# Four transformer layers on one core: the same operations in another written-out order, with fewer and longer bursts of small matrix products

## The chip, the core and the metric

The kernel runs on one NeuronCore of a Trainium2 chip. A core has a matrix engine (TensorE, in the profile PE, its weight loads PEld), a vector engine (VectorE, DVE), a scalar engine (ScalarE, ACT), a general engine (GpSimd, POOL) and a queue that starts DMAs (SyncE, SP). Each engine works through its own queue in order; semaphores tie the queues together. SBUF is the on-chip memory of 128 partitions, PSUM the eight banks into which PE writes. The metric is the device time of the whole program in microseconds.

## The reference

The input x has 2048 tokens of width 448. Two kinds of layer alternate, A B A B, each with a layer norm ahead and a residual sum behind:

```python
# A: 16 heads of width 28, each token looks at 8 tokens: itself and 7 at steps of 2 back
qkv = (x @ wqkv).reshape(B, S, 3, H, Dh)
idx = pos[:, None] - (arange(8) * 2)[None, :]
logits = einsum("bhsd,bhswd->bhsw", q, kg) * Dh**-0.5   # masked where idx < 0
o = einsum("bhsw,bhswd->bhsd", softmax(logits), vg)
return o @ wo
# B: gated, F = 1792
h = (x @ w_gate) * (x @ w_up)
return h @ w_down
```

All inputs and the output are bf16. Both A layers share their weights, and both B layers theirs.

## The kernel before, in words

Tokens lie in SBUF so that those of even and of odd place form the two halves of the token axis; a step of 2 back is then a step of 1 inside a half. A layer is worked in chunks of 256 or 512 tokens (`CH`, `SEQ`), and the chunks of neighbouring layers overlap: layer 1 begins while layer 0 still has chunks to do.

**Layer norm** (`ln_chunk`): DVE takes the statistics (L578, L580), ACT makes 1/sqrt (L581, L583), DVE normalises (L599). The transposition goes by PE (L609, L613) with an evacuation on ACT or DVE (L620, L623) in layer 0, and by DMA later.

**Projections** (`qk_chunk`, `v_group`): whole products of 64 rows by 128 columns, in pairs that fill the two halves of the array. All whole products are issued at L347. Evacuations of q and k are L708, of v L773 to L800; the `ORDER` list decides whether ACT or DVE does each.

**Attention** (`attn_front`, `attn_back`): the query blocks (17 of 120 or 128 queries) go in 9 groups, one of one block and eight of two. For a group of two, PE makes 32 + 32 small score products (L831; half as many where the tiles are 64 by 64), ACT takes the exponential (L841), DVE puts the band mask on (L848). Then PE makes 32 + 32 small value products (L866; 16 + 16 for the single block), whose results are copied (L880, ACT or DVE), added (L884), and normalised: a shuffle of the sums on DVE (L894), logarithm and exponential on ACT (L895, L896), the product on DVE (L907). The output projection and residual sum follow (`y_blocks`, L924). The small products use tiles of 64 rows by 32 columns; the scores of the first six groups of layer 0 use 64 by 64.

**The gated layer** (`b_chunk`): 14 hidden units of 128 features for each chunk. A unit is seven pairs of whole products (gate and up), an ACT copy of the gate (L960) and a DVE product with the up half (L963). The down projection is again in pairs at L347, its residual sum is L924; the last two token blocks use L975 and L979.

**What sets the order.** Nothing is planned when the program is built. `ORDER` (L101) is a written list of operation numbers for each engine, and `BANKS` (L163) names the PSUM banks of each PE operation. `schedule` (L222) reads both; it adds a wait on the operation that empties a bank to the next one that takes it. `emit` (L271) issues the queues and sets a semaphore wait where an operation reads what another engine wrote. An entry of the PE list such as

```python
"805+806*845/3/2"
```

is a **burst with strips**: the small products of operations 805 and 806 are issued together, and three of the seven steps of the whole operation 845, from its third step on, are spread between them. Those steps are then not one pair of products of 128 columns but eight products of 32 columns at four places in each half of the array, issued at L350 (`pair`, L342), so that the tiling does not change inside the burst. `cut_of` (L359) cuts the small products into parts of eights around the strips. An entry that is one number, such as `866`, is issued as it stands; `a+b*c/k/f` gives the bursts a and b, the host c, its strip steps k, and the step f from which they are taken.

Of the kernel before, what the change touches and what calls it, by code (L numbers as in the profile page):

```python
# [93 lines left out]
def grp_nc(g):  # L94
# [22 lines left out]
    ),  # L117
    "act": (
# [12 lines left out]
    ),  # L131
    "dve": (
# [18 lines left out]
    ),  # L151
    "pool": (
        "21 24 39 28 23 18 29 35 40 25 36 26 20 32 44 33 37 19 27 22 41 34 38 42 30 65 43 31 63"
# [952 lines left out]
```

## Time and profile before

| | us |
|---|---|
| median of 3 runs | 384.64 |
| lowest, highest | 384.35, 386.83 |
| the profiled execution | 384.78 |
| its span in the trace | 382.8 |
| PE busy | 377.2 |
| DVE busy | 288.7 |
| ACT busy | 197.2 |

The span runs from the first to the last instruction of the trace; the profiled execution took 2.0 us more than that. "Busy" is the time in which at least one instruction of an engine ran. For PE the ends of matmuls are modelled, so that starts are the better guide to what a product costs; the timeline view gives them. In the grouped views a row has the line, engine, operation, tiles and shapes, the count, then the busy time and the mean duration in ns, and behind the second bar the idle time of the engine ahead of it with what ended it.

### The profile page before, as it was taken

The numbers are of one execution on the slowest core, as the hardware profiler recorded it, in microseconds if no ns is written. First come the engines' busy times: TensorE is split into PE (matmuls) and PEld (weight loads), VectorE is DVE, ScalarE is ACT, GpSimd is POOL, SyncE is SP. The second block draws the span as 40 slices with busy tenths as digits, with TensorE's granted clock in tenths as the row PEclk, the third lists the DMA queues.
The fourth block names the chain that finished last, engine by engine and source line by source line (L and its number), as shares of the span: only waits on it lengthen the run. The fifth ranks groups of instructions, "written<-read, shape, count | busy, mean of one in ns | idle before, by whom it ended". The sixth has DMA issues, their size and how long they took to land.

```text
span 382.8 us, 14279 instructions
## 1 busy us (share of the span) xinstructions
PE 377.2 (99%) x6338; PEld 210.8 (55%) x6338; DVE 288.7 (75%) x652; ACT 197.2 (52%) x383; POOL 7.1 (2%) x33
## 2 busy tenths in 40 slices
PE   8999999999999999999999999999999999999997
PEld 3655577544454545446766666555555444445665
DVE  7998999998756876897567888668899687174443
ACT  4897887566426356156456236448653534125220
POOL 6000000000000000000000000000000000000000
PEclk9999999999999999999999999999999999999999
DMA  7665542700421030232001214320124002313004
GB/s 251 171 161 135 122 116 65 105 3 2 81 39 39 11 56 19 50 62 47 6 15 38 50 29 76 73 36 8 35 46 75 2 3 60 64 23 38 2 2 134
DMA packets 54880, 22.49 MB, mean 59 GB/s; under 512 B 45012, under 2 KB 54820, under 8 KB 54820
## 3 DMA queue, kind: packets, MB, share of 16 engines
q1 hardware_dynamic: 54676, 21.53, 26.5%
q8 instruction: 50, 0.82, 0.9%
q14 instruction: 10, 0.08, 0.1%
q10 hardware_dynamic: 144, 0.06, 0.1%
HBM read 8.54 MB, written 2.71 MB: 29 GB/s over the span
## 4 chain that ended last, share of the span: by engine, by line
PE 89%; DVE 6%; DMA 1%; ACT 1%; issue 1%; SPq 0%; DVEq 0%
PE ps L347 81%; PE ps L350 3%; PE ps L831 2%; PE ps L866 2%; PE ps L975 1%; DVE st L578 1%; DMA xnTb<-xn_sb 1%; DVE xn_sb L599 1%; DVE E_sb L848 1%; DVE x_sb L924 1%; DMA x_sb<-in_A_x_dram 1%; DVE oT L907 0%; PE ps L613 0%; DVE hT L963 0%; DVE R_sb L894 0%
## 5 line engine op out<-in xcount | busy, mean ns | idle before, releaser
L347 PE MATMUL ps<-xnTb,WGU 64*128 64x512 bf16 (+1 forms) x1900 | 173.7, 332 | 0.3
L347 PEld LDWEIGHTS ps<-xnTb,WGU 64*128 64x128 bf16 x1900 | 92.4, 94 | 71.5 <-ACT g_sb L960 1.5
L960 ACT ACTIVATE g_sb<-ps 128x512 bf16<-128x512 f32 (+1 forms) x140 | 69.0, 509 | 112.4 <-PE ps L347 93.8
L963 DVE TENSOR_TENSOR hT<-g_sb,ps 128x512 bf16<-128x512 bf16 (+1 forms) x140 | 77.7, 573 | 43.2 <-ACT g_sb L960 41.8
L347 PE MATMUL ps<-WD,hT 64*128 64x448 bf16 x802 | 83.5, 349 | 0.1
L347 PEld LDWEIGHTS ps<-WD,hT 64*128 64x128 bf16 x802 | 38.5, 94 | 33.4 <-DVE hT L963 0.5
L347 PE MATMUL ps<-xnTa,WQK 64*128 64x512 bf16 (+1 forms) x486 | 52.7, 352 | 0.6 <-issue 0.3
L924 DVE TENSOR_TENSOR x_sb<-x_sb,ps 128x448 bf16<-128x448 bf16 x62 | 36.8, 611 | 18.2 <-PE ps L347 18.1
L841 ACT ACTIVATE E_sb<-ps,shift_sb 128x1024 bf16<-128x1024 f32 (+1 forms) x36 | 37.5, 1068 | 11.6 <-PE ps L831 11.4
L578 DVE BATCH_NORM_STATS2 st<-x_sb 128x6 f32<-128x448 bf16 x64 | 38.5, 615 | 1.5 <-DMA x_sb<-in_A_x_dram 1.3
L599 DVE TENSOR_SCALAR xn_sb<-x_sb,mv,rstd 128x512 bf16<-128x512 bf16 (+1 forms) x64 | 35.1, 567 | 4.7 <-ACT rstd L583 4.5
L347 PEld LDWEIGHTS ps<-xnTa,WQK 64*128 64x128 bf16 x486 | 23.4, 94 | 18.4 <-issue 0.4
L708 ACT ACTIVATE qk<-ps 128x1024 bf16<-128x1024 f32 (+1 forms) x28 | 25.7, 929 | 8.7 <-PE ps L347 6.1
L347 PE MATMUL ps<-wo_g,oT 64*128 64x448 bf16 x256 | 29.5, 350 | 0.1
L895 ACT ACTIVATE R_sb<-R_sb 128x480 f32<-128x480 f32 (+1 forms) x34 | 19.9, 601 | 15.7 <-DVE R_sb L894 15.6
L848 DVE TENSOR_TENSOR E_sb<-E_sb,MK 128x1024 bf16<-128x1024 bf16 (+1 forms) x36 | 23.1, 656 | 5.2 <-ACT E_sb L841 5.2
L907 DVE TENSOR_TENSOR oT<-O_sb,R_sb 128x480 bf16<-128x480 f32 (+3 forms) x36 | 21.8, 624 | 6.5 <-ACT R_sb L896 6.5
L347 PE MATMUL ps<-WV,xnTa 64*128 64x336 bf16 (+3 forms) x252 | 23.3, 304 | 0.0
L894 DVE STREAM_SHUFFLE R_sb<-O_sb 128x480 f32<-128x480 f32 (+1 forms) x34 | 22.8, 691 | 0.0
L896 ACT ACTIVATE R_sb<-R_sb 128x480 f32<-128x480 f32 (+1 forms) x34 | 19.9, 599 | 0.2
L347 PEld LDWEIGHTS ps<-wo_g,oT 64*128 64x128 bf16 x256 | 12.1, 94 | 11.1 <-DVE oT L907 0.7
L866 PEld LDWEIGHTS ps<-E_sb,v_sb 64*32 64x32 bf16 x1088 | 12.6, 90 | 8.2 <-issue 3.6
(61 smaller groups left out, 215.4 us busy)
## 6 DMA issues: line engine op xcount, KB each, us to landing
out_dram<-x_sb SPq DMA_DIRECT2D x15, 112.0 KB, 1.8
x_sb<-in_A_x_dram SPq DMA_DIRECT2D x3, 448.0 KB, 5.7
hT<-in_A_wqkv_dram SPq DMA_DIRECT2D x4, 224.0 KB, 4.8
WGU<-in_B_w_gate_dram SPq DMA_DIRECT2D x4, 224.0 KB, 4.0
WGU<-in_B_w_up_dram SPq DMA_DIRECT2D x4, 224.0 KB, 4.4
WD<-in_B_w_down_dram SPq DMA_DIRECT2D x2, 448.0 KB, 4.9
WGU<-in_B_w_gate_dram SPq DMA_DIRECT2D x2, 336.0 KB, 4.6
WGU<-in_B_w_up_dram SPq DMA_DIRECT2D x2, 336.0 KB, 4.4
```

The source lines that it names most:

```text
L347: return lambda E: E.matmul(out(), lhs(), rhs(), start=start, stop=stop)
L578: sc.add("dve", one(lambda E, B=B: E.bn_stats(st6[:, B, :], x_sb[:, B, :]), ("bn", li, B)), 525.0, deps=[("x", li - 1, B)] + ([("xn", li - ...
L599: sc.add("dve", one(lambda E, B=B, dst=dst, src=src: E.tensor_scalar(dst, src, mv[:, B, 0:1], rstd[:, B:B + 1], ALU.subtract, ALU.mult), ( ...
L708: return E.activation(dst, src, ACT.Copy) if hasattr(E, "activation") else E.tensor_copy(dst, src)
L841: return E.activation(E_sb[:, slot, 2 * hp:2 * hp + 2, 0:w], ps[:, b0:b0 + 2, 0:w], ACT.Exp, bias=shift_sb[:, 0:1], scale=SCALE)
L848: return E.tensor_tensor(e, e, MK[:, kind, 0:nc].unsqueeze(1).unsqueeze(1).to_broadcast([128, 2, w // nc, nc]), ALU.min)
L866: parts[eb // 2].append((lambda E, b=b, c=c, o=o, vw=vw, eb=eb, eo=eo: E.matmul(ps[32 * b:32 * b + 32, bk[c], o:o + nc], vw, E_sb[64 * c:6 ...
L894: sc.add("dve", one(lambda E: E.stream_shuffle(R_sb[:, rs, 0:w], O_sb[:, os_, 0:w], [DH] * 32), ("Rs", li, qb)), dve_est(w) + 20.0, deps=[ ...
L907: return E.tensor_tensor(oT[:, :, a % HALF:a % HALF + z - a], O[:, :, a - tok:z - tok], R_sb[:, rs, 0:w].rearrange("p (h n) -> p h n", h=4 ...
L924: sc.add("dve", one(lambda E: E.tensor_tensor(x_sb[:, B, :], x_sb[:, B, :], ps[:, bk[w], 0:D], ALU.add), ("x", li, B)), dve_est(D), deps=[ ...
L960: sc.add("act", one(lambda E, gs=gs, bk=bk: E.activation(g_sb[:, gs, 0:nt], ps[:, bk[0], 0:nt], ACT.Copy), ("G", li, j, fc)), act_est(nt), ...
L963: sc.add("dve", one(lambda E, gs=gs, bk=bk, fc=fc: E.tensor_tensor(hT[:, fc, hs, 0:nt], g_sb[:, gs, 0:nt], ps[:, bk[1], 0:nt], ALU.mult), ...
```

## The change

The lists `ORDER` and `BANKS` are replaced; no other line differs. The program issues the same operations. What is different:

- PE's queue. Small products stand in 38 bursts instead of 45. The value products of three and of four blocks now stand in one burst (one of 96 and two of 128 products, at most 64 before), with five or seven strip steps between. In all there are 54 strip steps instead of 58. Some bursts mix score and value products in both kernels. The places of projections, hidden units, and output products between the bursts move too.
- DVE's and ACT's queues follow another order, and 43 evacuations change between the two engines. DVE has 11 of the 36 q and k copies (8 before), 5 of the v copies of L800 (8 before) and 17 of the 36 first copies of value sums (14 before).
- SP's queue of DMAs is in another order; so are the PSUM banks. GpSimd's queue is the same.

From the diff of `ORDER`'s PE list (the other lists are replaced in the same way):

```diff
-        "805+806*845/3/2 863 857 869 848 875 860 872 922 881 923 935 940 936 941 916 1003 917 920 1015 1006 921 1012 918 818 919 1027 819 1024 1039 1018 1036 "
-        "854 1030 946+947*866/2/1 878 884 952 1009 953 970+971*885/2/5 890 886 1042 887 1021 891 965 892 976 1033 977 893 966 1045 1061 1064 1070 1046 1067 1073 "
...
-        "1234 1240 1104 1237 1185+1186*1105/3/4 1167 1168*1106/2 1306 1310 1307 1311 1252 1308 1191+1192*1312/2 1309 1313 1330 1180 1331 1181 1341+1342*1246/2/5 "
+        "805+789+806+790*860/5 845 857 869 881 863 872 920 922 921 923 935 918 875 916 936 919 917 1012 1003 940 1006 941 1024 946*854/1/6 947 866 1018 1015 818 "
+        "1030 819 952+953*878/2/5 1027 1009 1036 1039 884 1021 970+971*885/2 890 886 887 976+977*891/2/4 1033 892 1042 893 1064 1070 1067 965 1061 1073 966 1045 "
...
+        "1234 1228 1185+1186*1105/2/1 1106 1231 1243 1240 1306 1312 1191+1167+1192+1168*1307/3/1+1313/4 1246 1252 1255 1308 1258 1309 1310 1237 1311 1330 1180 "
```

Here 789, 790 and 805, 806 are the value products of the first group (one block) and the second group (two blocks) of layer 2, whose 96 products now stand in one burst; 1167, 1168 and 1191, 1192 are those of its groups 4 and 5, now 128 products in one burst.

122 rows, old and new, of tables (BANKS, ORDER) are left out of this document.

## The prediction

> **What bounds the kernel now.** I read the page first: the span, the busy shares, the slices and the chain that ended last.
>
> ```profile
> span 382.8 us, 14279 instructions
> PE 377.2 (99%) x6338; PEld 210.8 (55%) x6338; DVE 288.7 (75%) x652; ACT 197.2 (52%) x383; POOL 7.1 (2%) x33
> ...
> DVE  7998999998756876897567888668899687174443
> ...
> PE 89%; DVE 6%; DMA 1%; ACT 1%; issue 1%; SPq 0%; DVEq 0%
> PE ps L347 81%; PE ps L350 3%; PE ps L831 2%; PE ps L866 2%; PE ps L975 1%; DVE st L578 1%; DMA xnTb<-xn_sb 1%; DVE xn_sb L599 1%; DVE E_sb L848 1%; DVE x_sb L924 1%; DMA x_sb<-in_A_x_dram 1%; DVE oT L907 0%; PE ps L613 0%; DVE hT L963 0%; DVE R_sb L894 0%
> ```
>
> PE is busy for 99% of the span and makes 89% of the chain, so the time is the sum of PE's work. But DVE's slices are nearly full for the first quarter, so I then asked for busy time by stretches (columns: stretch, its length, then busy us and instruction count of each engine):
>
> ```profile
> 12.00:95.00 83.00, 81.96 (x1692) 47.78 (x1690) 79.15 (x197) 63.10 (x115) 0.00 (x0) 1.00 0.42 90
> 95.00:300.00 205.00, 204.90 (x3614) 114.14 (x3612) 155.43 (x334) 103.25 (x200) 0.00 (x0) 1.00 0.23 42
> ```
>
> From 12 to 95 us PE and DVE are both full: DVE has 83.00 - 79.15 = 3.85 us to spare, and PE's idle of 83.00 - 81.96 = 1.04 us is where it already waits. From 95 to 300 us PE is idle for 0.1 us and DVE has 49.6 us to spare: there only PE's own order counts, and the waits of an order that leaves too little between a product and its reader. The granted clock is 1.00 in both.
>
> "Busy" hides what a burst of small products costs, since the ends of matmuls are modelled. I therefore read starts in the timeline (start, busy us, line, shape, count). A single value burst between whole products:
>
> ```profile
> 157.73 0.92 PE L347 MATMUL ps<-WD,hT 64*128 64x448 bf16 x8
> 158.58 0.34 PE L866 MATMUL ps<-E_sb,v_sb 64*32 64x72 bf16 x32
> 158.86 0.82 PE L347 MATMUL ps<-xnTb,WGU 64*128 64x512 bf16 x6
> ```
>
> Whole products go in pairs. Four pairs of 448 columns last 0.92 us, and the last one of them is its own 0.35 us long, so they start (0.92 - 0.35)/3 = 0.19 us apart and the next pair was due at 157.73 + 4 x 0.19 = 158.49. The burst starts at 158.58: 0.09 us to change over. The next pair starts at 158.86, so **32 value products alone cost 0.37 us**, of which some 0.2 us are the two changes of tiling. Now 64 of them in one burst, first bare, then with four strip steps between (a strip step is one pair of a whole product, cut into eight products of 32 columns at L350):
>
> ```profile
> 42.90 0.92 PE L347 MATMUL ps<-WV,xnTa 64*128 64x448 bf16 x8
> 43.75 0.71 PE L866 MATMUL ps<-E_sb,v_sb 64*32 64x64 bf16 x64
> 44.40 0.61 PE L347 MATMUL ps<-xnTa,WQK 64*128 64x256 bf16 x8
> ```
>
> ```profile
> 131.22 0.73 PE L347 MATMUL ps<-wo_g,oT 64*128 64x448 bf16 x6
> ...
> 132.16 0.21 PE L866 MATMUL ps<-E_sb,v_sb 64*32 64x64 bf16 x8
> 132.19 0.40 PE L350 MATMUL ps<-xnTa,WQK 64*32 64x512 bf16 x8
> 132.41 0.24 PE L866 MATMUL ps<-E_sb,v_sb 64*32 64x64 bf16 x16
> ...
> 133.11 0.60 PE L347 MATMUL ps<-xnTa,WQK 64*128 64x512 bf16 x4
> ```
>
> Bare, the next pair was due at 43.66 and starts at 44.40: 0.74 us, exactly twice the single burst, so putting two together bare gains nothing. With strips the next pair was due at 131.22 + 3 x 0.19 = 131.79 and starts at 133.11, 1.32 us later. A strip step takes 132.41 - 132.19 = 0.22 us. The row of whole products of 512 columns says the same for a pair (126.2 us over 558 pairs = 0.226), so a strip step costs nothing of its own:
>
> ```profile
> L347 PE MATMUL ps<-xnTb,WGU 64*128 64x512 bf16 x1116 | 126.2, 376 | 0.2
> ```
>
> That leaves 1.32 - 4 x 0.22 = **0.44 us for 64 value products with strips**, and eight products take 132.19 - 132.16 = 0.03 us there. Strips are what makes a merger pay: 0.30 us for two bursts. Score products, single and as 64 with two strip steps:
>
> ```profile
> 145.02 0.92 PE L347 MATMUL ps<-WD,hT 64*128 64x448 bf16 x8
> 145.87 0.33 PE L831 MATMUL ps<-Qz,qk 64*32 64x80 bf16 x32
> 146.13 1.88 PE L347 MATMUL ps<-WD,hT 64*128 64x448 bf16 x18
> 147.94 0.29 PE L831 MATMUL ps<-Qz,qk 64*32 64x64 bf16 x24
> ...
> 148.78 0.36 PE L347 MATMUL ps<-WD,hT 64*128 64x448 bf16 x2
> ```
>
> Single: 146.13 - (145.02 + 0.76) = 0.35 us. Sixty-four: due at 146.13 + 9 x 0.19 = 147.84, next at 148.78, less 2 x 0.19 of strips: 0.56 us against 0.70 for two.
>
> **The change part by part.** Only the written-out order and the PSUM bank list differ; every product is still computed. I counted the bursts in both programs' PE queues. Of bursts in 32-column tiles, before has 12 single value bursts, 1 bare one of 64, 8 of 64 with strips, 8 single score bursts, 6 score bursts of 64, and 2 mixed ones of 128 and 96 products. After has 7 single value bursts (one directly behind a score burst, sharing a change), 6 of 64 (five with two strip steps, one with one), 1 of 96, 2 of 128, 4 single score bursts, 8 of 64, and 3 mixed ones of 96, 64 and 64. The 64-column score bursts at the start fall from 8 to 7. In all 45 bursts become 38, and 58 strip steps become 54, so "more strips" holds for a burst, not for the sum; by the strip step's price that is worth nothing.
>
> Prices for forms that the trace lacks: 96 and 128 products lie between 0.2 for the changes plus 0.03 for each eight (0.56 and 0.68) and as many bare singles (1.11 and 1.48). They carry five and seven strip steps, so I take 0.62 and 0.78, near the low end, since a burst of 64 with few strips is nearer to that than to the bare one. The mixed ones go the same way (96: 0.62, 128: 0.78, 64: 0.55). Sixty-four values with two strip steps lie between 0.44 and 0.74: 0.50; with one: 0.62.
>
> The eight bursts of 64 with strips have two to seven of these; for them I take 0.46, between the 0.44 quoted and 0.50. Before: 12 x 0.37 + 0.74 + 8 x 0.46 + 8 x 0.35 + 6 x 0.56 + 0.78 + 0.62 = 16.42 us. After: 7 x 0.37 - 0.10 + 5 x 0.50 + 0.62 + 0.62 + 2 x 0.78 + 4 x 0.35 + 8 x 0.56 + 0.62 + 2 x 0.55 = 15.39 us. With one early burst fewer (its two changes, 0.2 us) **PE's work shrinks by 1.2 us**; the bounds are 1.7 us (17 changes of tiling fewer, 94 against 77, at 0.1 us each, with perfect packing) and a loss of 0.7 us (if the three longest bursts pack like bare ones, 1.9 us dearer: 1.11 - 0.62 + 2 x (1.48 - 0.78)).
>
> One rule speaks against strips: the Trainium skill's page "TensorEngine Tiling (Array Packing)", Restrictions, says that column tiling switches fast weight loading off, and its page "TensorE: Matmul & The Clock Gate", LDWEIGHTS, gives columns/1.2 ns for a load. By that the eight loads of a strip step take 0.21 us in turn, an estimate, which is 0.02 us over a 448-column step; by it both kernels would pay some 0.5 us and the sum would stay within 0.1 us. The trace, with 0.22 us for a 512-column strip and 0.03 us for eight loads and products together, does not show it.
>
> **Waits in the first stage.** 83 us in which DVE has 3.85 us to spare are the place where an order can lose more than it gains. The evacuations that change engine there cost on DVE:
>
> ```profile
> L708 DVE CAST qk<-ps 128x1024 bf16<-128x1024 f32 x6 | 7.3, 1214 | 1.5 <-PE ps L347 1.5
> L800 DVE CAST v_sb<-ps 128x672 bf16<-128x672 f32 x8 | 6.8, 847 | 0.3 <-PE ps L347 0.2
> L708 DVE CAST qk<-ps 128x512 bf16<-128x512 f32 x2 | 1.4, 678 | 0.0
> ```
>
> In layer 0, two full qk copies (chunk 2 part 2, chunk 3 part 0) move onto DVE, 2 x 1.21 = 2.43 us. One full and one half copy and two v copies move off, 1.21 + 0.68 + 2 x 0.85 = 3.59 us; small copies of transposes and value sums come on for nearly the same amount. The sum stays about level, but what comes on is early and what goes off is later, so DVE is up to 2.4 us deeper in the middle of the stage. Behind those copies in DVE's queue stand masks, Qz and the normalisation for which PE waits. The bounds are +2.4 us (all of it reaches PE) and -1.0 us (the idle that PE has now goes). I take **+0.2 us**: the sum is level, and ACT, which takes the other copies, has 83.00 - 63.10 = 19.9 us free.
>
> **Waits in the later stages.** Here a single score burst shows what a short cover costs now:
>
> ```profile
> 282.38 1.50 PE L347 MATMUL ps<-WD,hT 64*128 64x448 bf16 x14
> 283.83 0.59 PE L831 MATMUL ps<-Qz,qk 64*32 64x64 bf16 x32
> 284.35 0.93 PE L347 MATMUL ps<-WD,hT 64*128 64x448 bf16 x8
> ```
>
> Due at 282.38 + 7 x 0.19 = 283.71, next at 284.35: 0.64 us instead of 0.35, so 0.29 us of waiting inside it. In the new order the score burst of layer 2's group 4 stands inside the last hidden unit of layer 3's 256-column chunk, five pairs behind the unit whose bank it takes. PE's cover is 5 x 0.11 + 0.09 + half a burst, 0.3 = 0.94 us; the chain is the drain, the ACT copy and the DVE product:
>
> ```profile
> L960 ACT ACTIVATE g_sb<-ps 128x256 bf16<-128x256 f32 x56 | 20.5, 383 | 32.4 <-PE ps L347 31.6 <-DVE hT L963 0.5
> L963 DVE TENSOR_TENSOR hT<-g_sb,ps 128x256 bf16<-128x256 bf16 x56 | 22.2, 415 | 18.2 <-ACT g_sb L960 17.1 <-PE ps L347 0.8
> ```
>
> 0.38 + 0.42 plus about 0.3 for drain and hand-overs: 1.1 us, so 0.2 to 0.4 us late. I find four or five such places in the new order (around 182, 220, 231 and 274 us) against three or four in the old. I take **+0.6 us**, between 0 and +1.6 (four more of 0.4).
>
> **The sum.** -1.2 + 0.2 + 0.6 = -0.4 us. The profiled execution took 384.78 us (382.8 of span and 2.0 around it), the median of three runs is 384.64; from the median, **384.2 us**.
>
> **The rivals.** First, the bursts pay in full and the first stage loses its waits too: -1.7 - 1.0 + 0 = -2.7, **381.9 us**. For it speaks that all 17 changes are PE's own time; against it that DVE stays as full as it was.
>
> Second, slower: DVE binds in the first stage. The two early qk copies push back the masks and normalisations, PE waits 2.4 us there, -1.2 + 2.4 + 1.6 = **387.4 us** with the tight later places. It decides against the change as soon as more than 0.6 us of those 2.4 reach PE beside the 0.6 later. For it speaks 79.15 of 83.00 us; against it the level sum.
>
> Third, the merged bursts end several groups at once, and their evacuation holds PE:
>
> ```profile
> L894 DVE STREAM_SHUFFLE R_sb<-O_sb 128x480 f32<-128x480 f32 x32 | 21.3, 689 | 0.0
> L907 DVE TENSOR_TENSOR oT<-O_sb,R_sb 128x480 bf16<-128x480 f32 x30 | 19.0, 650 | 4.5 <-ACT R_sb L896 4.4
> L963 DVE TENSOR_TENSOR hT<-g_sb,ps 128x512 bf16<-128x512 bf16 x84 | 55.8, 679 | 25.0 <-ACT g_sb L960 24.8
> ```
>
> Four query blocks bring DVE 4 x (0.69 + 0.65) = 5.4 us at once. In 5.4 us PE finishes 3.5 hidden units of 1.55 us (seven pairs), whose DVE products need 3.5 x 0.68 = 2.4 us. If DVE took the blocks first, PE would lose up to 2.4 us at each of two bursts: 384.2 + 4.8 = **389.0 us**. The same page on tiling, PSUM Bottleneck, warns that evacuation may become the limit once tiling has sped PE up. Against it: DVE has 49.6 us to spare from 95 to 300 us, and its queue interleaves the blocks with hidden products.
>
> Fourth, the longer bursts pack like bare ones: -0.4 + 1.9 = +1.5, **386.1 us**. For it speaks that no burst over 64 of one kind stands in the trace; against it that their strips come after every 16 products, as in the quoted one.
>
> **How the numbers follow.** Forecast 0.58, the first rival 0.12, the second 0.14, the third 0.07, the fourth 0.09. Faster by over 1% would need -3.8 us, more than all bounds together: 0.03. Slower by over 1% is the third rival and the upper end of the second: 0.10. Within 1%, about what a measurement of this kernel can tell from no change: 0.87. The range reaches to the first and the second rival and takes in the fourth, 381.8 to 387.6 us.
>
> **What would show it.** Value bursts of 96 and 128 at 0.6 to 0.8 us beside their strips, strip steps at 0.22 us; in the stretch 12 to 95 us PE's idle near 1.0 us and DVE near 79 us; bursts with 0.2 to 0.4 us of waiting around 182, 220 and 231 us. I am wrong if PE's idle in the first stage grows by over a microsecond, or if a whole product stands still behind a burst of 128.

## The result and the profile after

| | before | after |
|---|---|---|
| median, us (14 runs each) | 384.57 | 387.44 |
| lowest, highest | 384.08, 386.83 | 385.19, 388.93 |
| the profiled execution | 384.78 | 386.76 |
| its span | 382.8 | 385.0 |
| last start of a product on PE | 380.18 | 381.38 |

The changed kernel takes 1.0066 times as long (95% interval 1.0050 to 1.0083), 1.9 to 3.2 us more where 0.4 us less were forecast. The last row of the table, a start read in the timeline, splits the 2.2 us between the two spans: PE ends 1.2 us later, and what follows its last product takes 3.66 us instead of 2.64, 1.0 us more.

The page of after, in the lines that were shown of before:

```profile
span 385.0 us, 14220 instructions
PE 377.1 (98%) x6314; PEld 210.7 (55%) x6314; DVE 290.2 (75%) x653; ACT 195.4 (51%) x382; POOL 7.3 (2%) x33
...
PE 88%; DVE 6%; DMA 2%; ACT 2%; issue 1%; SPq 1%; DVEq 0%; ACTq 0%
PE ps L347 80%; PE ps L350 3%; PE ps L831 2%; PE ps L866 2%; PE ps L975 1%; DMA WV<-in_A_wqkv_dram 1%; DVE hT L963 1%; DMA xnTb<-xn_sb 1%; DVE x_sb L924 1%; DVE st L578 1%; DVE xn_sb L599 1%; SPq L440 1%; PE ps L613 0%; DVE E_sb L848 0%; DVE Qz L819 0%
```

PE is as busy as before to 0.1 us (377.1 against 377.2), in a longer span. In the chain SPq, SP's issuing of DMAs, stands at 1% instead of 0%, now with its line L440 (the outputs), and DMA at 2% instead of 1%. The busy times of the two long stretches of after (stretch, length, then busy us and count of PE, PEld, DVE, ACT, POOL; granted clock, DMA share, GB/s):

```profile
12.00:95.00 83.00, 80.45 (x1686) 46.65 (x1682) 74.54 (x185) 61.70 (x112) 0.00 (x0) 1.00 0.42 90
95.00:300.00 205.00, 204.90 (x3596) 114.22 (x3594) 160.19 (x346) 99.33 (x195) 0.00 (x0) 1.00 0.23 42
```

PE's idle in the first stage is 83.00 - 80.45 = 2.55 us against 1.04, and DVE is less busy than before, 74.54 us against 79.15. So PE waits more there, and not for a fuller DVE.

**The bursts.** PE's timeline of after around one of the bursts of 128:

```profile
256.87 1.67 PE L347 MATMUL ps<-xnTa,WQK 64*128 64x512 bf16 x14
258.47 0.25 PE L866 MATMUL ps<-E_sb,v_sb 64*32 64x64 bf16 x16
258.54 0.40 PE L350 MATMUL ps<-xnTa,WQK 64*32 64x512 bf16 x8
258.75 0.24 PE L866 MATMUL ps<-E_sb,v_sb 64*32 64x64 bf16 x16
...
260.68 1.69 PE L347 MATMUL ps<-xnTb,WGU 64*128 64x512 bf16 x14
```

Seven pairs start (1.67 - 0.38)/6 = 0.215 us apart, so the next one was due at 258.38; it starts at 260.68, and 2.30 less seven strip steps of 0.215 are 0.79 us, where the prediction had put 0.78. The other burst of 128 took 0.91, that of 96 took 0.69. Added up in this way, with the waits inside them, all bursts cost some 1.1 us less than before (23.2 against 22.1; the sum depends by about 0.1 us on how the edges of a burst are read).

**The standstill at 75.8 us.** PE's timeline of before, then of after, where layer 1's second chunk begins:

```profile
75.67 0.93 PE L347 MATMUL ps<-wo_g,oT 64*128 64x448 bf16 x8
76.73 1.47 PE L347 MATMUL ps<-xnTb,WGU 64*128 64x512 bf16 x12
```

```profile
75.39 0.73 PE L347 MATMUL ps<-WV,xnTa 64*128 64x336 bf16 x8
77.43 0.82 PE L347 MATMUL ps<-xnTb,WGU 64*128 64x512 bf16 x6 [1.30 <-DMA xnTb<-xn_sb]
```

In after the array runs empty for 1.30 us, and the first product starts 1.46 us later than it was due (0.29 before). The releaser is a DMA, the transposition of the normalised rows; the trace has the last landing of these four transposes 0.05 us ahead of the start, at 77.38 us, and before at 76.68. So the 1.17 us more have two parts: the data come 0.70 us later, and PE comes 0.47 us earlier (due at 75.97 us instead of 76.44), only to wait for them. DVE's timeline of after shows when these rows were made, and the timeline of SP's queue when their transposes were issued:

```profile
63.64 0.73 DVE L599 TENSOR_SCALAR xn_sb<-x_sb,mv,rstd 128x896 bf16<-128x896 bf16 x1
64.42 0.73 DVE L599 TENSOR_SCALAR xn_sb<-x_sb,mv,rstd 128x896 bf16<-128x896 bf16 x1
...
69.40 1.39 DVE L599 TENSOR_SCALAR xn_sb<-x_sb,mv,rstd 128x896 bf16<-128x896 bf16 x2
```

```profile
65.39 1.09 SPq L728 DMA_TRANSPOSE v_sb<-vt  x1
66.53 0.82 SPq L717 DMA_DIRECT2D vt<-qk  x2
67.39 2.02 SPq L728 DMA_TRANSPOSE v_sb<-vt  x1
69.46 2.64 SPq L602 DMA_TRANSPOSE xnTb<-xn_sb  x2
72.14 0.47 SPq L717 DMA_DIRECT2D vt<-qk  x1
72.66 3.05 SPq L602 DMA_TRANSPOSE xnTb<-xn_sb  x2
```

The same two views of before:

```profile
65.84 0.73 DVE L599 TENSOR_SCALAR xn_sb<-x_sb,mv,rstd 128x896 bf16<-128x896 bf16 x1
67.02 0.72 DVE L599 TENSOR_SCALAR xn_sb<-x_sb,mv,rstd 128x896 bf16<-128x896 bf16 x1
```

```profile
65.97 1.09 SPq L728 DMA_TRANSPOSE v_sb<-vt  x1
67.11 3.79 SPq L602 DMA_TRANSPOSE xnTb<-xn_sb  x2
70.94 0.82 SPq L717 DMA_DIRECT2D vt<-qk  x2
71.81 3.19 SPq L602 DMA_TRANSPOSE xnTb<-xn_sb  x2
```

Here a spill (L717) is a DMA from SBUF to the scratch tensor `vt` in DRAM, and a v copy (L728) is a transposing DMA that reads it back. In after the first two row blocks were ready at 64.37 and 65.15 us, but a v copy, two spills and a second v copy stood ahead of their transposes in SP's queue, which issues in order. A transposing DMA mostly holds the queue for 1.1 to 1.3 us, a spill for 0.3 to 0.5, and the second v copy held it for 2.02. So the first transpose went out at 69.46, 4.3 us after the second block. In before the blocks were ready later, at 66.57 and 67.74, and the first went out at 67.11.

**The end.** What line L440 of the source issued from 375.6 us on, before and after (shortest, median and longest issue in ns, then the first and the last start):

```profile
L440 SPq DMA_DIRECT2D out_dram<-x_sb x11: 332/455/458, 375.7 to 380.9; - x11
```

```profile
L440 SPq DMA_DIRECT2D out_dram<-x_sb x11: 332/453/1712, 376.9 to 383.0; - x11
```

Eleven outputs stand in a row in both, but in after one issue takes 1712 ns instead of 455. The last sum is done at 382.06, and the last output is issued only at 382.96, when the row before it is through; before, the last output went out at once. The DMA view of the same 7.4 us of after has a third queue that before's does not have in that time:

```profile
q1 hardware_dynamic: 1165, 0.93, 37.5%
q10 hardware_dynamic: 144, 0.06, 2.8%
q8 instruction: 1, 0.02, 0.9%
```

It is an instruction fetch, whose packet moves at 377.5 us; the long issue starts at 377.26. After issues 24 matrix products and 24 weight loads fewer on PE (four strip steps fewer) and reaches the end 1.2 us later, and its last fetch lies at 377.5 us instead of 374.0, in the middle of the outputs.

### The profile page after: what moved, and what is told of

Same layout as the page of the kernel before. It is cut to its first block, busy times and chain, and to the rows that moved or that the text cites. A ratio compares the mean times of both kernels' runs of the same rounds, so it can differ in the third digit from the quotient of the medians.

```text
span 385.0 us, 14220 instructions
## 1 busy us (share of the span) xinstructions
PE 377.1 (98%) x6314; PEld 210.7 (55%) x6314; DVE 290.2 (75%) x653; ACT 195.4 (51%) x382; POOL 7.3 (2%) x33
## 4 chain that ended last, share of the span: by engine, by line
PE 88%; DVE 6%; DMA 2%; ACT 2%; issue 1%; SPq 1%; DVEq 0%; ACTq 0%
PE ps L347 80%; PE ps L350 3%; PE ps L831 2%; PE ps L866 2%; PE ps L975 1%; DMA WV<-in_A_wqkv_dram 1%; DVE hT L963 1%; DMA xnTb<-xn_sb 1%; DVE x_sb L924 1%; DVE st L578 1%; DVE xn_sb L599 1%; SPq L440 1%; PE ps L613 0%; DVE E_sb L848 0%; DVE Qz L819 0%
## 5 line engine op out<-in xcount | busy, mean ns | idle before, releaser
L963 DVE TENSOR_TENSOR hT<-g_sb,ps 128x512 bf16<-128x512 bf16 (+1 forms) x140 | 77.4, 574 | 34.6 <-ACT g_sb L960 34.2
L347 PE MATMUL ps<-WD,hT 64*128 64x448 bf16 x800 | 81.9, 349 | 0.1
L578 DVE BATCH_NORM_STATS2 st<-x_sb 128x6 f32<-128x448 bf16 x64 | 38.1, 615 | 0.8 <-DMA x_sb<-in_A_x_dram 0.7
L708 ACT ACTIVATE qk<-ps 128x1024 bf16<-128x1024 f32 (+1 forms) x25 | 22.0, 901 | 6.5 <-PE ps L347 4.5
L581 ACT ACTIVATE lnv<-mv,eps_sb 128x2 f32<-128x2 f32 (+1 forms) x33 | 9.4, 292 | 19.2 <-DVE mv L580 19.0
L708 DVE CAST qk<-ps 128x1024 bf16<-128x1024 f32 (+1 forms) x11 | 12.8, 1168 | 6.6 <-PE ps L347 4.9
```

The source lines that it names most:

```text
L347: return lambda E: E.matmul(out(), lhs(), rhs(), start=start, stop=stop)
L578: sc.add("dve", one(lambda E, B=B: E.bn_stats(st6[:, B, :], x_sb[:, B, :]), ("bn", li, B)), 525.0, deps=[("x", li - 1, B)] + ([("xn", li - ...
L708: return E.activation(dst, src, ACT.Copy) if hasattr(E, "activation") else E.tensor_copy(dst, src)
L963: sc.add("dve", one(lambda E, gs=gs, bk=bk, fc=fc: E.tensor_tensor(hT[:, fc, hs, 0:nt], g_sb[:, gs, 0:nt], ps[:, bk[1], 0:nt], ALU.mult), ...
```

## The experiments

The theory after the two traces: both losses sit in SP's queue, 1.2 us at the transposes and 1.0 us at the outputs. Its rivals are that the standstill at 75.8 us is paid for anyway by the next wait, that the fetch beside the long issue is a coincidence, and that the bursts gave less than they seem to. Ten kernels were run in three lots, each against the kernel before on the same chip; microseconds worked out from ratios take 1% as 3.85 us. By their 95% intervals a difference between two of these ratios is known to 0.7 to 1.0 us. A profile shows one execution, and the executions of one kernel spread over 1.5 to 4.4 us: a wait that one profile shows is not yet the kernel's.

### Transposes first

```diff
-529 601 596 534 445 447 599 449 451 606 605
+529 445 447 601 596 449 451 599 534 606 605
```

This is SP's list of after; 445, 447, 449, 451 are the transposes, 596 to 601 spills, the others v copies. The edit moves the first two transposes ahead of two spills and the v copy 534, the last two ahead of a third spill and 534; the v copy 529 stays ahead of all.

> The changed kernel with one edit in SP's list: the four transposing DMAs of layer 1's second chunk (445, 447, 449, 451) go ahead of two v copies and two spill DMAs that stand before them, which nothing needs before about 83 us. Theory S (SP's queue is late): the normalised blocks were ready at 65.2 us and their transpositions were issued only at 69.5 us, so PE's standstill of 1.46 us at 75.8 us falls to 0.3 us or less, and the time falls by about 1.2 us against the changed kernel, to some 385.9 us. Rival D (DVE's order in the first stage sets when the blocks are ready): the last two blocks are normalised at 70.8 us whatever SP does, the last landing moves by less than 0.4 us, and the time falls by less than 0.4 us.

Measured: ratio 1.0046 (1.0030 to 1.0062), median 386.43. By the ratios that is 0.8 us less than the changed kernel, known to 0.9, so this run alone does not show a gain. SP's and PE's timelines of this kernel:

```profile
67.52 3.37 SPq L602 DMA_TRANSPOSE xnTb<-xn_sb  x2
70.94 0.82 SPq L717 DMA_DIRECT2D vt<-qk  x2
71.81 2.57 SPq L602 DMA_TRANSPOSE xnTb<-xn_sb  x2
```

```profile
76.90 1.47 PE L347 MATMUL ps<-xnTb,WGU 64*128 64x512 bf16 x12 [0.17 <-DMA xnTb<-xn_sb]
```

The standstill is 0.34 us instead of 1.46, but the edit cannot be credited with that. Of the fall, 0.53 us are an earlier start (76.90 instead of 77.43), the other 0.59 PE's coming later in this execution. And the kernels of the next two sections, whose list is here that of after, start at 76.77 and 76.53 us, with standstills of 0.77 and 0.74. The two queues of the first of them:

```profile
66.41 1.09 SPq L728 DMA_TRANSPOSE v_sb<-vt  x1
67.55 3.38 SPq L602 DMA_TRANSPOSE xnTb<-xn_sb  x2
```

```profile
76.77 1.47 PE L347 MATMUL ps<-xnTb,WGU 64*128 64x512 bf16 x12 [0.61 <-DMA xnTb<-xn_sb]
```

With the list unedited the transposes went out at 67.55 us, 1.9 us ahead of after. In after's execution three spills at 62.52 us took 2.82 us together (1.16 in this one), and the second v copy 2.02 (1.09), each beside an instruction fetch. The late issue in after's profile thus comes from the list and from where fetches fell, and these profiles do not divide it. With the edit the standstill was 0.34 us here, and 0.92 and 0.99 in two later kernels.

The profiled execution, the slowest of the twelve, also has a new standstill of 0.9 us at 295 us, and the end lies 4.13 us behind PE's last start, with one output of 2.18 us beside a fetch.

### Outputs in the order in which their rows are ready

```diff
-1577 1575 1481 1567 1559 1479 1285 1277 1283 1565 1557 1487 1489 1622 1628
+1577 1575 1481 1479 1285 1277 1283 1487 1489 1567 1565 1559 1557 1622 1628
```

> The changed kernel with one edit at the end of SP's list: the output DMAs in the order in which their rows are ready, so that nine of the eleven no longer queue behind the one that waits for token block 11. Theory S: the last output is issued at once after the last sum (0.05 us after 382.06 us instead of 0.9 us), the span ends 0.85 us earlier and the time falls by about 0.85 us. Rival: the end is set by the last DMA's own way to memory, as in the kernel before, and the time stays within 0.2 us.

Measured: ratio 1.0033 (1.0013 to 1.0053), median 385.78, 1.3 us below the changed kernel. PE's last product starts at 380.60 and the span ends 2.65 us later, as before: the 1.0 us at the end are gone. (PE's being 0.8 us earlier than in after's profile is not the edit's, which lies behind 346 us; most of it is the shorter standstill at 76 us.) Only four outputs are left for the last 7 us; with that room the last one goes out at once, at 381.31. A fetch still lies among them, at 376.7 us, but the issue beside it takes 0.33 us.

### Four more strip steps

```diff
-1341+1342*1264/2/5
+1341+1342*1264/4/3
-1365+1366*1267/2/5
+1365+1366*1267/4/3
```

SP's queue stays as in after; PE's two score bursts take four strip steps instead of two, so that PE runs as many instructions as before the change.

> The changed kernel with four whole steps cut into strips more (two score bursts at about 282 and 298 us with four strip steps instead of two), so that PE has again as many instructions as in the kernel before (24 matmuls and 24 weight loads more). No work differs. By the price of a strip step (nothing of its own) PE's work stays the same within 0.1 us. Theory F (an instruction fetch that falls on SP's output DMAs holds one of them for 1.3 us): the last fetch moves 48 instructions, some 2.3 us, ahead, out of the row of outputs, no output DMA takes 1.7 us to issue, and the time falls by about 0.85 us. Rival: the long issue belongs to the DMA that is second in the row, or to chance, stays, and the time is the same within 0.2 us. If strip steps cost something, the time rises.

Measured: ratio 1.0036 (1.0018 to 1.0054), median 386.23, 1.2 us below the changed kernel. The last fetch is back at 374.2 us, and line L440 from 375.6 us on reads

```profile
L440 SPq DMA_DIRECT2D out_dram<-x_sb x11: 332/453/458, 376.0 to 381.2; - x11
```

No issue is long, the last one starts at 381.2, and the end is 2.65 us behind PE, with the outputs in after's order. A change on PE has mended a queue on SP, by moving a fetch.

### The mirror: the fetch put into the kernel before

```diff
-1371+1372*1271/7
+1371+1372*1271/3
```

In the kernel before the change one value burst of 64 takes three strip steps instead of seven, so PE runs 48 instructions fewer.

> The kernel before with four strip steps taken out of its last long value burst (seven of every ten... strips reduced from seven to three), so that TensorE runs 48 instructions fewer and its last instruction fetch comes about 2.3 us later, at about 376.3 us, inside the row of output issues. Theory (a fetch holds the SP issue beside it by about 1.3 us): one output issue of 1.6 to 1.8 us in place of 0.45, the last output issued about 0.85 us late (1.28 less the 0.42 us that the queue had to spare), the time 0.8 to 0.9 us longer, ratio 1.002. Rival (the fetch is a coincidence, and strip steps cost or give nothing): all issues at 0.45 to 0.5 us, the time unchanged within 0.2 us.

Measured: ratio 1.0027 (1.0014 to 1.0039), 1.0 us slower. Line L440 and the DMA view from 375.6 us on, in this kernel:

```profile
L440 SPq DMA_DIRECT2D out_dram<-x_sb x11: 332/451/1913, 376.6 to 382.8; - x11
```

```profile
q8 instruction: 1, 0.02, 1.3%
```

The fetch now lies at 377.5 us, one issue takes 1913 ns, and the span ends 3.84 us behind PE's last start. With four strip steps a kernel can be moved into this loss and out of it. All six profiles in which the outputs stand in a row agree: where an instruction packet lies in that time (after, the first experiment, this one), one output takes 1.7 to 2.2 us; where none does (before, four more strip steps, late transposes), the longest takes 0.46 or 0.47. In the six kernels that have only four outputs left there, a packet lies in that time too, and no issue is long but one of 1.16 us.

### Late transposes in the kernel before

```diff
+    scratch = nc.dram_tensor("scratch", (512, 128), bf, kind="Internal").ap()
+    for i in range(4):
+        plain_dma("sp", scratch[128 * i:128 * i + 128, :], ident[:], ("extra", i), "d_extra", deps=["c_id"])
...
-533 447 445
+533 1629 1630 1631 1632 447 445
```

Four DMAs whose copies nothing reads stand ahead of the transposes in SP's queue.

> The kernel before with four small DMAs of 32 KB to a scratch tensor put into SP's list ahead of the same four transposing DMAs; nothing reads them. They take SP about 0.5 us each, so the transpositions are issued some 2 us later. Theory S: PE, which now stands still for 0.29 us at 76.2 us, stands for 2.0 us or a little less, and the time rises by 1.2 to 2.0 us. Rival D: SP has slack there and the time rises by less than 0.4 us.

Measured: ratio 1.0044 (1.0028 to 1.0060), 1.7 us slower. SP's and PE's timelines:

```profile
66.87 3.36 SPq L440 DMA_DIRECT2D scratch<-ident  x4
70.28 2.58 SPq L602 DMA_TRANSPOSE xnTb<-xn_sb  x2
72.91 0.83 SPq L717 DMA_DIRECT2D vt<-qk  x2
73.78 2.67 SPq L602 DMA_TRANSPOSE xnTb<-xn_sb  x2
```

```profile
78.16 1.04 PE L347 MATMUL ps<-xnTb,WGU 64*128 64x512 bf16 x8 [1.29 <-DMA xnTb<-xn_sb]
```

The four issues take 3.4 us, where 2 were expected. Issued even later than in after, the transposes make the same standstill in the old order, 1.45 us instead of 0.29, and PE's last product starts 1.3 us later. So late transposes do cost PE this time. The four copies also moved 128 KB, which this run does not separate from the time that their issue takes.

### Both edits of SP's queue together

This kernel is the changed kernel with the first two edits, "transposes first" and "outputs in the order in which their rows are ready". The kernels of the next sections have them too.

> The changed kernel with both edits of SP's queue: the transposes of layer 1's second chunk issued as soon as their rows are ready, and the outputs issued as their rows become ready. Theory (the loss sits in SP's queue): the two gains stand at different places and add, 0.8 + 1.3 us off 387.1, so about 385.0 us, ratio 1.001; what is left above before is the first stage's and the later waits' 0.3 to 0.6 us against 1.2 us that the bursts save. Rival (one of the two gains was only the other's, since an instruction fetch that misses one row of issues hits the other): no better than the outputs' edit alone, 385.8 us, ratio 1.003.

Measured: ratio 1.0006 (0.9992 to 1.0021), median 385.16, 2.3 us below the changed kernel, which is clear of the noise. The two gains add, 0.8 + 1.3 against 2.3 us, as far as each is known. Against the outputs' edit alone the transposes' edit gives 1.0 us, just clear of the noise; this profile's standstill of 0.92 us does not show where. With another order of the same DMAs, the new order of PE, DVE and ACT is no longer measurably slower.

### The long bursts split

```diff
-805+789+806+790*860/5 845
+805+806*860/3 789+790*845/2
-1191+1167+1192+1168*1307/3/1+1313/4
+1191+1192*1307/3/1 1167+1168*1313/3/1
-1371+1347+1348+1372*1272/7 1273
+1371+1347*1272/4 1348+1372*1273/4
```

> The changed kernel with both edits of SP's queue, and its three longest value bursts (96, 128 and 128 products) split again into bursts of 32 and 64: 41 bursts in place of 38, as many strip steps. Theory (the bursts save as they were priced): the split bursts cost 2.7 us in sum against 2.4, each burst more 0.1 to 0.2 us, so 0.3 to 0.5 us more than the kernel with both edits alone. Rival (long bursts give nothing, since their products wait for the weights' evacuation at their ends): the same time within 0.2 us, or less.

Measured: ratio 1.0032 (1.0021 to 1.0044), 1.0 us above the kernel with both edits alone. The two halves of the burst shown above, in PE's timeline of this kernel (rows of whole products):

```profile
257.33 1.68 PE L347 MATMUL ps<-xnTa,WQK 64*128 64x512 bf16 x14
...
259.98 0.39 PE L347 MATMUL ps<-xnTa,WQK 64*128 64x512 bf16 x2
...
261.35 0.82 PE L347 MATMUL ps<-xnTb,WGU 64*128 64x512 bf16 x6
```

Due at 257.33 + 7 x 0.217 = 258.85, next at 259.98, less three strip steps (0.65): 0.49 us; again due at 260.20, next at 261.35: 0.50. Together 0.99 us for what the one burst does in 0.79. Over the three places the split bursts cost 2.89 us against 2.34, so the bursts explain 0.55 of the 1.0 us. The profiled execution has two more standstills for DMAs, 0.23 us at 246 and 0.27 at 296, that the unsplit one has not. Long bursts save what they were priced at; the rival, that they give nothing, falls.

### The copies back on their engines

Four q and k copies of layer 0 go back to the engine that they had before the change: two full ones from DVE to ACT, a full and a half one from ACT to DVE.

> The changed kernel with both edits of SP's queue, and the four evacuations of the first layer that changed engine put back on the engines they had before (two copies of q and k from VectorE to ScalarE, two the other way). Theory (the first stage's added waits, 0.25 us, are waits for VectorE): 0.2 to 0.3 us less than the kernel with both edits alone. Rival (VectorE binds nothing there): the same time within 0.2 us, since VectorE's sum in the first stage is 74.5 us against 79.2 before.

Measured: ratio 1.0014 (1.0001 to 1.0028), median 385.09 against 385.16 without this edit. No gain shows, as the rival had it, but the 0.2 to 0.3 us that were expected are less than the 0.8 us that these two ratios can tell apart. In the profiled execution the standstill at 75.7 us is gone, but a new one of 0.53 us stands at 65.8.

### The four transposes in one row, and three waits moved

```diff
-529 445 447 601 596 449 451 599 534
+529 445 447 449 451 601 596 599 534
```

> The changed kernel with both edits of SP's queue, and the four transposes of layer 1's second chunk now issued as one row, the two spills of layer 0 behind them instead of between. In the kernel with both edits TensorE still stood still for 0.92 us at 75.7 us, and the two spills take 0.82 us of SP's queue ahead of the third transpose. Theory (the issue in SP's queue sets the transposes' landing): the standstill falls to 0.1 to 0.3 us and the time by 0.5 to 0.8 us against the kernel with both edits, about 384.5 us, ratio 0.999. Rival (the landing waits for the transfer itself and the instruction fetch beside it): standstill unchanged, same time within 0.2 us.

Measured: ratio 1.0012 (0.9998 to 1.0025), median 385.09: no gain over 1.0006, the rival's side. The standstill was 0.58 us here and 0.34 in the profile of the next kernel, which has the same list, against 0.92; a new one of 0.60 us stands at 66 us here. What limits is seen by putting the runs side by side, end of the last transpose's issue and restart of PE: 75.71 and 77.43 (after), 74.37 and 76.90 (transposes first), 73.99 and 76.74 (both edits), 73.86 and 76.99 (this one), 73.16 and 76.42 (the next kernel). An issue 2.55 us earlier brings a restart only 1.01 us earlier. In each of them the last landing comes 0.05 us ahead of the restart, so it is the way from the issue to the landing that gets longer, from 3.5 us after the start of the last issue (after) to 4.5 (the next kernel). Why it does was not tried.

The next kernel has this list, and three neighbours in DVE's queue change places:

```diff
-1051 880
+880 1051
-1292 1084
+1084 1292
-1420 1269
+1269 1420
```

1051, 1292 and 1420 are a norm's statistics (L578), 880 an evacuation of a value sum, 1084 and 1269 hidden products (L963).

> As the run with the four transposes in one row, and three pairs of neighbours in VectorE's queue change places, so that what TensorE waits for goes ahead of statistics that nothing waits for yet: the evacuation of a value sum ahead of a norm's statistics at 198.5 us, a hidden product ahead of statistics at 229.1 and at 283.0 us. Theory (the later stages' added waits are such places, 0.13 + 0.12 + 0.26 us): 0.4 to 0.5 us less than without the three, about 384.0 us, ratio 0.998, and below before by a part of what the bursts save. Rival (each wait moves to the next reader): the same time within 0.2 us.

Measured: ratio 0.9996 (0.9980 to 1.0012), median 384.67. That is 0.6 us below the run before it, within the 0.8 us that the two ratios leave open, so the time decides neither for the theory nor for the rival. One of the three places, in the timelines of after and of this kernel:

```profile
283.20 1.15 DVE L578 BATCH_NORM_STATS2 st<-x_sb 128x6 f32<-128x448 bf16 x2
...
284.27 0.67 DVE L963 TENSOR_TENSOR hT<-g_sb,ps 128x512 bf16<-128x512 bf16 x1
284.99 1.44 PEld L347 LDWEIGHTS ps<-WD,hT 64*128 64x128 bf16 x18 [0.54 <-DVE hT L963]
```

```profile
283.17 0.69 DVE L963 TENSOR_TENSOR hT<-g_sb,ps 128x512 bf16<-128x512 bf16 x1 [0.18 <-ACT g_sb L960]
283.77 0.62 DVE L578 BATCH_NORM_STATS2 st<-x_sb 128x6 f32<-128x448 bf16 x1
283.91 1.06 PEld L347 LDWEIGHTS ps<-WD,hT 64*128 64x128 bf16 x14 [0.29 <-DVE hT L963]
```

In after two statistics stand ahead of the hidden product; the gate's copy is done at 283.98 us, and the product starts 0.3 us after it. With one of them behind it the standstill of 0.26 us at 285 us is gone, and so is that of 0.11 at 231 us; at 200 us 0.13 us stay. With all edits the new order stands where before stood; no kernel here beats before by more than the measurement can tell.

## Why the prediction was wrong

The sum had three terms, -1.2 + 0.2 + 0.6. The traces give, from the starts of whole products against their distances of 0.19 or 0.22 us, as sums over the rows of the timeline:

| | predicted | measured, us |
|---|---|---|
| bursts | -1.2 | -1.1 |
| waits, 12 to 95 us | +0.2 | +1.6 |
| waits, 95 to 310 us | +0.6 | +0.65 |
| start, to 12 us | - | +0.2 |
| behind PE's last product | - | +1.0 |
| sum | -0.4 | +2.3 |

At the start, the first long row of projections begins at 11.42 us instead of 11.25. The spans differ by 2.2 us, so 0.1 us has no place. The measured time, 387.4 us, lies inside the range by the way of the second rival alone, whose mechanism did not occur.

- **Bursts: right.** The forms that the trace of before lacked came out at 0.69 us (96 products; 0.62 predicted), 0.79 and 0.91 (128; 0.78), and the split run, 1.0 us slower, confirms 0.55 us of it on the bursts themselves. Other single prices missed by more: the mixed burst of 128 in before took 1.09 us (0.78 put), the mixed one of 96 in after 0.90 (0.62), the value burst with one strip step 0.75 (0.62). That they nearly cancel in the difference is luck. The fourth rival, long bursts that pack like bare ones, falls: 0.79 is far from 1.48. The strip step is 0.21 to 0.22 us here too.
- **Later waits: right in size.** They grew from 0.43 to 1.08 us. Of the four places named, that at 231 us was right; the others turned up at 138, 200, 227 and 285 us (0.18, 0.12, 0.16 and 0.26 us), of which the one at 285 us comes from neighbours in DVE's queue that the prediction had not read.
- **The first stage: the step that failed.** It asked only whether DVE's sum grows, and took +0.2 us. The second rival had the right time, 387.4 us, by luck: its reason was wrong, for DVE's sum fell by 4.6 us, and putting the copies back brought no gain that shows. PE's idle did grow by 1.5 us, which the prediction had named as what would make it wrong. Of the 1.6 us, 1.46 - 0.29 = 1.17 are the one standstill at 75.8 us, a wait for DMAs. The prediction said nothing of SP's queue, though the change put it in another order: its cost stood at nothing, without the work that would hide it. Nor did it ask what PE waits for when the saved burst time brings it there early: 0.47 of the 1.17 us are time won ahead of a landing that does not come sooner. The other 0.70 us are a later landing. That late transposes cost PE this is shown in the old order; how much of the 0.70 the new list makes and how much the fetches beside SP's issues in the profiled execution stays open, since two profiles with the same list have the landing as early as before. That the transposes now stand behind two spills and a v copy more was to be read in the two lists, and what each of these holds the queue for in the old trace.
- **The end: not in the sum at all.** The order of the outputs looked harmless, since eleven of them stand in a row in both kernels. It is harmless with 0.4 us to spare, and not when one issue takes 1.3 us more. That the fetch would fall elsewhere followed from the four strip steps fewer, 48 instructions, which the prediction counted and priced at nothing. The price of a long issue stood in before's trace, and its cause could be read there: from 95 us on nine of SP's issues are long, and each of the nine has an instruction packet beside it. The first transpose of the standstill at 76 us, too, took 2.4 us, with a packet at 67.9 us.
- **Third rival: no.** No whole product stands still behind a burst of 128; the next pair at 260.68 starts a row of 14 without a wait.

## What to carry to other kernels

When an order changes, read the queue that issues DMAs as an engine: give each issue its duration, and compare when the data was ready with when its DMA went out. A queue that issues in order should hold DMAs in the order in which their data becomes ready, above all where PE waits next and at the end. Time saved on the busiest engine is lost again at the next landing that it has to wait for. And before an edit is credited with a wait that is gone from its profile, look at a second profile that has the old list at that place.

## What the runs showed of the hardware

An instruction fetch often lengthens the DMA issue beside it, which had not been expected. The 50 instruction packets of queue q8 move 0.82 MB, 16.4 KB each; where one falls into a row of output issues, an issue takes 1.7 to 2.2 us instead of 0.46, and beside the fetch at 68.0 us of after a transposing copy takes 2.02 us instead of 1.09. The twelve profiles together have 1263 issues of SP from 95 us on. Of these 149 are long (over 1.5 us for a transposing DMA, over 0.7 for a plain one), and 147 of the 149 overlap an instruction packet. Of the 1114 others, 130 overlap one: a fetch beside an issue does not always lengthen it, but a long issue nearly always has one. The Trainium skill's page "Runtime: NRT & Kernel Launch", Instruction fetch mechanics, gives blocks of 16 KiB and calls the crossing mostly hidden: the size agrees, but for the queue that issues DMAs the fetch was not hidden: 0.9 to 1.7 us more at each of the issues named here. Why the fetch of one engine holds SP's issue is not settled by these runs. The time of two kernels moved in this way with the mere number of their instructions: 1.0 us more in before with 48 fewer, 1.2 us less in after with 48 more.
